# A router, eight experts and a gated layer on one core: the low parts of all expert weights move to VectorE, the conversion of the float64 weights gets a plan, and the last layer begins with two token groups in turn

## The chip, the cores and the metric

The kernel runs on one core of a Trainium2 chip. The metric is the device time of one launch in microseconds, the median of several runs. Lower is better.

## The reference

Three layers follow each other: attention in which keys far below the row's maximum are masked out, a mixture of eight experts that sends each token to one expert, and a gated feed-forward layer. All is fp32, but the three weights of the last layer arrive as float64, because their scaling makes numpy widen them.

```python
# attention: B=4, H=8, S=576, D=64        -> x [2304, 512]
scores = scale * q @ k.T ; keep scores >= max - tau ; attn = softmax ; attn @ v
# experts: N=2304 tokens, D=512, E=8, F=1024
expert_idx = argmax(normalized(x) @ normalized(emb).T / tau)
for e in range(E):                          # tokens of that expert only
    h = maximum(x[mask] @ w1[e], 0.0)       # w1 [8, 512, 1024]
    out[mask] = gate_w[mask, None] * (h @ w2[e])   # w2 [8, 1024, 512]
# last layer: d_ff = 1536, weights float64
g = x @ w_gate ; val = x @ w_val
return (g * sigmoid(g) * val) @ w_out
```

## The kernel before

TensorE multiplies in a rounded fp32 form (F32R). To keep fp32 accuracy each operand is split into a high part (the rounded value, a ScalarE cast) and a low part (operand minus high part, a subtraction on VectorE or GpSimd), and each product is three matmuls: high by high, high by low, low by high.

**Attention** takes the first third of the span; the change does not touch it. During it and behind it the router sorts the tokens by expert in DRAM (`xs`), and the first 256 tokens of one expert are already done (`Early`).

**Experts** (`moe`). The experts are taken by their number of remaining tokens, the fullest first: rank r = 0 to 7 has room for 448, 368, 336, 304, 288, 256, 256 and 256 tokens (`CW`). A rank has eight slots, k = 0 to 7, one for each 128 columns of the hidden layer. In slot k `l1(r, k)` makes one hidden tile (12 matmuls), ScalarE and VectorE cut it into `hh` and `hl`, and `l2(r, k - 2)` adds the tile of two slots earlier to the four outputs (12 matmuls). The weights come in pieces of two slots: `wload(1, q)` and `wload(2, q)` fetch 512 KB each into one of two buffers, and `wsplit` makes the parts. ScalarE casts the high part; the low part of every w1 piece and of the first w2 pieces is made by GpSimd, the low part of w2 from piece 12 on (and of piece 0) by VectorE. The next rank's tokens are transposed in slots 5 and 6 (`xT`), and results go out by `yout` and `stores`. The order here is that of the code (`manual_schedule`).

**Float64 weights** (`Weights2`). The last layer's weights are 36 blocks (gate, value, out for each of 12 columns of d_ff), fetched as pairs of 32-bit words, 512 KB each. `split` converts one to fp32: a ScalarE scale, then three VectorE operations that put the words together (tile `wb`). `join` makes its high part (ScalarE) and its low part (GpSimd). `turn(i)` does some of it in slot i of the experts: it starts a load in every second slot until 18 blocks are fetched. What is left is done by `step`, three times per step of the last layer.

**Last layer** (`moe2`). Six groups of 384 tokens. A step (g, k) is `l1(g, k)`, 24 matmuls of 384 columns into `pg` and `pv`, then Silu on ScalarE, the product on VectorE, its split into `uh` and `ul`; and `l2` of the step before, nine matmuls of 512 columns into three output tiles. The steps go group by group, k = 0 to 11 in each. Before the change no order is fixed here: the framework's scheduler chooses it on every engine. `pg` and `pv` share five PSUM banks, the outputs have three. All loads of the kernel go through one queue (SP), in order; a load that waits for its buffer holds up those behind it.

Of the kernel before, what the change touches and what calls it, by code (L numbers as in the profile page):

```python
# [15 lines left out]
def f(ap):  # L16
    return ap.bitcast(F32)
# [1140 lines left out]
def moe(ctx, tc, attn, hp, w1, w2, xs, ti, yd, idl, ident):  # L1158
# [24 lines left out]
    def gate(r, *ts):  # L1183
        for t in ts or range(0, CW[r], 128):
            gated((nc.scalar, nc.vector)[t // 128 % 2], st[r]["xw"][0:min(128, CW[r] - t), t // 128, :])

    def wload(nm, q):
        r, fp = divmod(q, 4)
        e, sl = bass.ds(st[r]["e"], 1), slice(256 * fp, 256 * fp + 256)
        if nm == 1:  # L1190
            t = pw.tile([128, 4, 256], F32, tag="w1", name="w1r")
            src = w1[e, :, sl].rearrange("e (c p) f -> p (e c) f", p=128)
        else:
            t = pw.tile([128, 2, DM], F32, tag="w2", name="w2r")
            src = w2[e, sl, :].rearrange("e (k p) d -> p (e k) d", p=128)
        nc.sync.dma_start(t[:], src)
        raw[nm, q] = t

    def wsplit(nm, q):
        t = raw.pop((nm, q))  # L1200
        hi = pwh.tile(list(t.shape), F32R, tag=f"{nm}h", name=f"w{nm}h")
        lo = pwh.tile(list(t.shape), F32R, tag=f"{nm}l", name=f"w{nm}l")
# [3 lines left out]
        W[nm, q] = (hi, lo)  # L1206

    def xT(r, c):

# [100 lines left out]
    wload(1, 0)  # L1310
    wload(2, 0)
    wload(1, 1)
    wsplit(1, 0)
    w2s, y0 = yield
    pxw, px, ph = p("m_xw", 1), p("m_x", 1), p("m_h", 3)
    pps, psy = p("m_ps", 4, space=PSUM), p("m_py", 4, space=PSUM)
    wload(2, 1)
    wsplit(2, 0)
    for i in range(8 * NE):
        r, k = divmod(i, 8)  # L1320
        q = 4 * r + k // 2
        if k == 0 and r + 1 < NE:
            regs(r + 1)
            xload(r + 1)
        if k == 4:
            ids(r)
            if r + 1 < NE:
                gate(r + 1)
# [33 lines left out]

class Weights2:

    EARLY = 6
    NF = DF2 // 128

    def __init__(self, ctx, tc, wg, wv, wo):
        self.tc, self.nc = tc, tc.nc
        p = lambda n, b: ctx.enter_context(tc.tile_pool(name=n, bufs=b, reuse_waits="tile", side="right"))  # L1370
        self.pw, self.pr = p("n_w", 1), p("n_r", 2)
        self.src = {"g": wg.bitcast(I32), "v": wv.bitcast(I32), "o": wo.bitcast(I32)}
        self.W = {}
        self.todo = [(k, nm) for k in range(self.NF) for nm in "gvo"]
        self.raw, self.half = [], []

    def turn(self, i):

        early = 3 * self.EARLY
        n = 3 * self.NF - len(self.todo)  # L1380
        if n < early and i % 2 == 0:
            self.load()
        if i % 2 == 1:
            self.join()
        elif len(self.raw) > 1 or n >= early:
            self.split()

    def step(self):
        if self.todo:
            self.load()  # L1390
        self.split()
        self.join()

    def load(self):
        k, nm = self.todo.pop(0)
        src = self.src[nm]
        if nm == "o":
            src = src[128 * k:128 * k + 128, :].rearrange("p (c f) -> p c f", c=4)
        else:
            src = src[:, 256 * k:256 * k + 256].rearrange("(c p) f -> p c f", p=128)  # L1400
        r = self.pr.tile([128, 4, 128, 2], I32, tag="r", name="r" + nm)
        self.nc.sync.dma_start(r[:].rearrange("p c f t -> p c (f t)"), src)
        self.raw.append((k, nm, r))

    def split(self):
        if not self.raw:
            return
# [3 lines left out]
        b = self.pr.tile([128, 512], I32, tag="wb", name="wb")  # L1411
        stt = nc.vector.scalar_tensor_tensor


        nc.scalar.activation(f(H), f(H), AF.Copy, scale=2.0 ** -112)
        nc.vector.tensor_scalar(b[:], L, 29, None, op0=ALU.logical_shift_right)  # L1416
        stt(out=b[:], in0=H, scalar=3, in1=b[:], op0=ALU.logical_shift_left, op1=ALU.bitwise_or)  # L1417
        stt(out=b[:], in0=H, scalar=-2 ** 31, in1=b[:], op0=ALU.bitwise_and, op1=ALU.bitwise_or)  # L1418
        self.half.append((k, nm, b))

    def join(self):
        if not self.half:
            return
# [13 lines left out]
def parts_y(pool):  # L1437
    return [pool.tile([128, 4, GT], F32R, tag="y" + x, name="y" + x) for x in "hl"]
# [7 lines left out]
def moe2(ctx, tc, w2s, yd, idl, out, y0, py0, pys):  # L1446
# [13 lines left out]

    H, Y = {}, {0: y0}

    def l1(g, k):
# [12 lines left out]
        s = pu.tile([128, GT], F32, tag="s", name="s")  # L1476
        nc.scalar.activation(s[:, 0:n], res[0][:, 0:n], AF.Silu)  # L1477
        nc.vector.tensor_tensor(s[:, 0:n], res[1][:, 0:n], s[:, 0:n], op=ALU.mult)  # L1478
        uh = pu.tile([128, GT], F32R, tag="uh", name="uh")
        ul = pu.tile([128, GT], F32R, tag="ul", name="ul")  # L1480
        nc.scalar.copy(uh[:, 0:n], s[:, 0:n])  # L1481
        nc.vector.tensor_tensor(ul[:, 0:n], s[:, 0:n], f(uh[:, 0:n]), op=ALU.subtract)
        H[g, k] = (uh, ul)

    O = {}

# [20 lines left out]
                in_=o[:], in_offset=None, bounds_check=NTOK - 1, oob_is_err=False)  # L1507
            apart(tc, "out", ins)

    seq = [(g, k) for g in range(len(groups)) for k in range(NF)]  # L1510
    for i, (g, k) in enumerate(seq):
        if w2s.todo:
            for _ in range(3):
                w2s.step()
        if g + 1 < len(groups):
            if k == 2:
                raw = pr.tile([128, 4, GT], F32, tag="yr", name="yr")
                nc.sync.dma_start(raw[:], yd[:, GT * (g + 1):GT * (g + 2)].rearrange("(c p) n -> p c n", p=128))
                Y[g + 1] = parts_y(py if g % 2 == 0 else py0)
            if k in (5, 6, 7, 8):  # L1520
                split_y(nc, Y[g + 1], k - 5, raw[:, k - 5, :])
        l1(g, k)
        if i:
            l2(*seq[i - 1])
            if seq[i - 1][1] == NF - 1:
                store(g - 1)
    l2(*seq[-1])
    store(len(groups) - 1)

# [35 lines left out]
def body(tc, q, k, v, tau, emb, mtau, w1, w2, wg, wv, wo, out):  # L1565
    nc = tc.nc
    with ExitStack() as top:
# [125 lines left out]
```

## Time and profile before

| | us |
|---|---|
| runs shown, median (lowest, highest) | 1085.92 (1081.8, 1086.0) |
| the profiled execution, its own time | 1089.41 |
| its span, first to last instruction | 1087.7 |
| granted TensorE clock over the span | 0.99 |
| TensorE busy | 1052.2 |
| VectorE, ScalarE, GpSimd busy | 583.1, 489.1, 375.0 |

Experts begin at 384.0 us of the span and the last layer at 625.3. Busy time of TensorE is modelled from pipelined matmuls, so a busy TensorE may still be slower than it could be; how far apart matmuls start tells more than how long one takes.

### The profile page before, as it was taken

To read this page: it belongs to the slowest core of one execution; us is meant where nothing else is said; L and a number is where in the kernel's file an instruction comes from. 1 tells how busy PE (TensorE), PEld (TensorE's weight loads), DVE (VectorE), ACT (ScalarE), POOL (GpSimd) and SP (SyncE) were. 2 spreads that over 40 slices of the span, in tenths; PEclk is the share of its full clock that TensorE was granted. 3 is DMA by queue.
4 is the path that set the end of the run, shared out by engine and by line. 5 is a ranking of instruction groups with operands and counts; after the bars stand their busy time and mean duration, and the time that the engine had idled before them with its cause. 6 is when DMAs were issued, how large, how long until landed. Compare 5 with 4: busy or idle time off the path is not lost.

```text
span 1087.7 us, 18328 instructions
## 1 busy us (share of the span) xinstructions
PE 1052.2 (97%) x6512; PEld 908.8 (84%) x6512; DVE 583.1 (54%) x1257; ACT 489.1 (45%) x1012; POOL 375.0 (34%) x414
## 2 busy tenths in 40 slices
PE   6999999999999689999999999999999999999997
PEld 5666676676668679999999998899999999999996
DVE  6877877888887335788964488421211211211211
ACT  5777777777773335565555454311211211211111
POOL 6444444455676355774643344110100100100101
PEclk9999999999999889999999999999999999999999
DMA  9678989755841477789897464100100100000000
GB/s 182 161 193 220 204 217 213 190 125 144 243 105 41 150 194 246 219 245 205 266 260 211 140 194 140 38 36 1 59 1 1 59 1 1 30 1 1 30 1 30
DMA packets 128574, 135.84 MB, mean 125 GB/s; under 512 B 52488, under 2 KB 94984, under 8 KB 128480
## 3 DMA queue, kind: packets, MB, share of 16 engines
q1 hardware_dynamic: 125600, 125.18, 43.4%
q0 software_dynamic: 2880, 9.46, 2.3%
q8 instruction: 53, 0.87, 0.3%
q14 instruction: 41, 0.34, 0.1%
HBM read 81.29 MB, written 27.77 MB: 100 GB/s over the span
## 4 chain that ended last, share of the span: by engine, by line
issue 39%; PE 11%; DMA 7%; POOL 3%; DVE 3%; ACT 1%; SPq 1%; POOLq 0%; ACTq 0%; DVEq 0%
PE ph L1248 5%; PE y L1266 5%; DMA w1r<-in_moe_w_dram 2%; DMA ro<-in_moe_w_out_dram 2%; DMA rg<-in_moe_w_gate_dram 2%; POOL w1l L1205 1%; POOL out_dram L1505 1%; DMA w2r<-in_moe_w_dram 1%; DVE wb L1417 1%; DMA rv<-in_moe_w_val_dram 1%; DVE wb L1418 1%; PE pxt L1217 1%; DVE wb L1416 0%; ACT w2h L1203 0%; POOL ol L1430 0%
## 5 line engine op out<-in xcount | busy, mean ns | idle before, releaser
L1478 DVE TENSOR_TENSOR s<-pv,s 128x384 f32<-128x384 f32 x72 | 40.1, 557 | 273.9 <-PE pv L1473 272.9
L1505 POOL DMA_INDIRECT out_dram<-os,idi x18 | 17.9, 994 | 378.2 <-DVE os L1503 374.5
L196 DVE TENSOR_REDUCE nmx<-PS 128x1 f32<-128x576 f32 x144 | 108.8, 756 | 58.1 <-PE PS L165 36.1
L1477 ACT ACTIVATE s<-pg 128x384 f32<-128x384 f32 x72 | 35.4, 491 | 181.4 <-PE pg L1473 181.4
L290 ACT COPY h<-PS 128x256 f32<-128x256 f32 (+2 forms) x176 | 67.2, 382 | 82.5 <-PE PS L247 81.1
L230 DVE SCALAR_TENSOR_TENSOR E<-PS,thr,E 128x576 f32<-128x576 f32 x128 | 103.5, 808 | 0.1
L1205 POOL TENSOR_TENSOR w1l<-w1r,w1h 128x1024 fp32r<-128x1024 f32 x32 | 80.8, 2525 | 52.1 <-ACT w1h L1203 52.1
L1481 ACT CAST uh<-s 128x384 fp32r<-128x384 f32 x72 | 37.0, 514 | 137.0 <-DVE s L1478 137.0
L220 ACT ACTIVATE E<-PS,nmx 128x576 f32<-128x576 f32 x128 | 96.4, 753 | 2.7 <-DVE nmx L196 0.8
L1473 PE MATMUL pg<-yh,gl 128*128 128x384 f32 x288 | 96.8, 336 | 0.0
L1473 PE MATMUL pg<-yh,gh 128*128 128x384 f32 x288 | 96.7, 336 | 0.0
L1473 PE MATMUL pg<-yl,gh 128*128 128x384 f32 x288 | 96.6, 336 | 0.0
L1473 PE MATMUL pv<-yh,vl 128*128 128x384 f32 x288 | 96.6, 335 | 0.0
L1473 PE MATMUL pv<-yh,vh 128*128 128x384 f32 x288 | 96.5, 335 | 0.0
L1473 PE MATMUL pv<-yl,vh 128*128 128x384 f32 x288 | 96.5, 335 | 0.0
L314 PE MATMUL y<-h,nv 128*64 128x320 f32 (+2 forms) x528 | 89.7, 422 | 0.0
L1496 PE MATMUL o<-oh,uh 128*128 128x512 f32 x216 | 85.0, 394 | 2.7 <-ACT uh L1481 2.7
L165 PE MATMUL PS<-KH,qs 128*128 128x288 f32 x256 | 86.1, 351 | 1.4 <-ACT h L290 1.2
L247 PE MATMUL PS<-ident,E 128*128 128x128 f32 x576 | 86.6, 277 | 0.6 <-DVE E L230 0.5
L1496 PE MATMUL o<-oh,ul 128*128 128x512 f32 x216 | 85.8, 397 | 0.0
L1496 PE MATMUL o<-ol,uh 128*128 128x512 f32 x216 | 85.3, 395 | 0.0
L247 PEld LDWEIGHTS PS<-ident,E 128*128 128x128 f32 x576 | 65.6, 140 | 22.3 <-issue 19.1
(328 smaller groups left out, 2577.2 us busy)
## 6 DMA issues: line engine op xcount, KB each, us to landing
w1r<-in_moe_w_dram SPq DMA_DIRECT2D x32, 512.0 KB, 6.5
w2r<-in_moe_w_dram SPq DMA_DIRECT2D x32, 512.0 KB, 5.1
xs<-zero SPq DMA_DIRECT2D x8, 1542.0 KB, 7.6
KH<-tkh SPq DMA_DIRECT2D x60, 144.0 KB, 2.6
KL<-tkl SPq DMA_DIRECT2D x60, 144.0 KB, 2.6
rg<-in_moe_w_gate_dram SPq DMA_DIRECT2D x12, 512.0 KB, 6.2
rv<-in_moe_w_val_dram SPq DMA_DIRECT2D x12, 512.0 KB, 8.3
ro<-in_moe_w_out_dram SPq DMA_DIRECT2D x12, 512.0 KB, 3.6
```

Source lines behind the costliest of these rows:

```text
L165: ins = nc.tensor.matmul(S[:, i, a:a + n], x, y, start=first, stop=last)
L196: nc.vector.tensor_reduce(nmx[:], S[:, :, 0:288], axis=AX.XY, op=ALU.max, negate=True)
L220: nc.scalar.activation(e, d["S", s][:, :, 0:288], AF.Exp, bias=d["nm", s][0][:], scale=1.0)
L230: nc.vector.scalar_tensor_tensor(out=e, in0=d.pop(("S", s))[:, :, 0:288], scalar=d.pop(("nm", s))[1][:], in1=e, op0=ALU.is_ge, op1=ALU.mul ...
L247: ins = nc.tensor.transpose(ps[:, o:o + 128], src, self.ident[:])
L290: self.tc.declare_no_dep(self.nc.scalar.copy(o, i).ins, group=f"new1_{g}", reason="the other bank")
L314: nc.tensor.matmul(ps[64 * b:64 * b + 64, p0:p1], v, self.H[i][:, k, o + p0:o + p1], start=c == 0, stop=c == 4 and (p1 == n or c0 == 0))
L1205: eng.tensor_tensor(lo[:], t[:], f(hi[:]), op=ALU.subtract)
L1248: nc.tensor.matmul(ps[:, 0:C], w[:, c, o:o + 128], x[:, c, 0:C], start=n == 0, stop=n == 11)
L1266: nc.tensor.matmul(d["y"][c][:, 0:C], w[:, k % 2, sl], h[:, 0:C], start=k == 0 and i == 0, stop=k == 7 and i == 2)
L1473: nc.tensor.matmul(ps[:, 0:n], w[:, c, :], y[:, c, 0:n], start=m == 0, stop=m == 11)
L1496: nc.tensor.matmul(O[g][t][:], u[:, sl], w[:].rearrange("p c f -> p (c f)"), start=k == 0 and i == 0, stop=k == NF - 1 and i == 2)
```

## The change

Three edits. (1) In `moe`, `wsplit` becomes `whigh` and `wlow`. The low parts are all VectorE's (but for the very first piece, which GpSimd still makes), and each is written a slot or a part of one behind its high part. The high part of the next w1 piece now stands behind `l1` of the slot, not ahead of it, and the next rank's gating stands behind both. (2) `Weights2` loads nothing in rank 0, keeps three blocks loaded ahead in a pool of their own with three buffers, and converts by plan: `begin` writes ScalarE's work on a block, `end` a slot later VectorE's. Two blocks in each of ranks 1 to 3 and one in each of ranks 4 to 7 are begun. In the last layer the same goes on, one block in even steps and two in odd ones, with the low parts on VectorE. (3) The last layer takes the first two groups in turn, two steps apart, so that each new block of weights serves two steps; its order on all engines is that of the code. `pg` and `pv` have two banks, the outputs six. A Silu of one column at the experts' end loads ScalarE's table ahead of time.

```diff
-    def wsplit(nm, q):
...
-        nc.scalar.copy(hi[:], t[:])
-        eng = nc.vector if (nm, q) == (2, 0) or nm == 2 and q >= 12 else nc.gpsimd
-        eng.tensor_tensor(lo[:], t[:], f(hi[:]), op=ALU.subtract)
+    def whigh(nm, q):
...
+            nc.scalar.copy(hi[:], t[:])
+    def wlow(nm, q, eng=nc.vector):
...
+            eng.tensor_tensor(lo[:], t[:], f(W[nm, q][0][:]), op=ALU.subtract)
...
+        if k % 2 == 0 and q + 2 < NQ:
+            wload(1, q + 2)
+        if k == 1:
+            wlow(1, q + 1)
+        l1(r, k)
         if k % 2 == 0:
-            if q + 2 < NQ:
-                wload(1, q + 2)
-            if q + 1 < NQ:
-                wsplit(1, q + 1)
-        l1(r, k)
+            whigh(1, q + 1)
+            wlow(2, q)
+        elif k > 1:
+            wlow(1, q + 1)
+        if k == 4 and r + 1 < NE:
+            gate(r + 1)
...
         if k % 2 == 1:
-            if q + 1 < NQ:
-                wsplit(2, q + 1)
+            whigh(2, q + 1)
...
+    nc.scalar.activation(one[:], ident[:, 0:1], AF.Silu)
     l2(NE - 1, 7)
...
     def turn(self, i):
+        r, k = divmod(i, 8)
+        if r and k % 4 == 0:
+            self.fill()
+        if r and k % 4 > 1 and (k < 4 or r < 4):
+            if k % 2 == 0:
+                self.begin(1)
+            else:
+                self.end()
...
+    def begin(self, n):
+        for _ in range(n):
+            if self.half:
+                self.high()
+            if self.raw:
+                self.scale()
...
-        nc.gpsimd.tensor_tensor(flat(lo), f(b[:]), f(flat(hi)), op=ALU.subtract)
+        self.lows.append(lambda: nc.vector.tensor_tensor(flat(lo), f(b[:]), f(flat(hi)), op=ALU.subtract))
...
-    pps, pso = p("n_ps", 5, space=PSUM), p("n_po", 3, space=PSUM)
+    pps, pso = p("n_ps", 2, space=PSUM), p("n_po", 6, space=PSUM)
...
         nc.scalar.activation(s[:, 0:n], res[0][:, 0:n], AF.Silu)
+        w2s.begin(1 + i % 2)
         nc.vector.tensor_tensor(s[:, 0:n], res[1][:, 0:n], s[:, 0:n], op=ALU.mult)
...
+        w2s.end()
+        w2s.fill()
...
-    seq = [(g, k) for g in range(len(groups)) for k in range(NF)]
+    LAG = 2
+    seq = [(0, k) for k in range(LAG)]
+    for k in range(NF):
+        seq += [(g, k + LAG - LAG * g) for g in range(2) if k + LAG - LAG * g < NF]
+    yload(1)
+    for c in range(4):
+        do[seq.index((1, 0)) - 2 + c // 2].append((ysplit, 1, c))
...
+            ctx.enter_context(tc.manual_schedule())
             moe2(ctx, tc, w2s, yd, idl, out, y0, py0, c)
```

VectorE in rank 7, the last expert, before the change (`hl` is the low part of a hidden tile, `w2l` that of a w2 piece; L1205 is `wsplit`):

```order
L1253 SCALAR_TENSOR_TENSOR hl<-ph,hh 128x256
L1205 TENSOR_TENSOR w2l<-w2r,w2h 128x1024
L1253 SCALAR_TENSOR_TENSOR hl<-ph,hh 128x256 x2
L1205 TENSOR_TENSOR w2l<-w2r,w2h 128x1024
L1253 SCALAR_TENSOR_TENSOR hl<-ph,hh 128x256 x2
```

And after it, from slot 1 to slot 4 of that rank (`w1l` is the low part of a w1 piece, `ol` that of a converted block, `wb` the three operations that put a block's words together; L1210 is `wlow`):

```order
L1210 TENSOR_TENSOR w1l<-w1r,w1h 128x1024
L1258 SCALAR_TENSOR_TENSOR hl<-ph,hh 128x256 x2
L1210 TENSOR_TENSOR w2l<-w2r,w2h 128x1024
L1258 SCALAR_TENSOR_TENSOR hl<-ph,hh 128x256
L1210 TENSOR_TENSOR w1l<-w1r,w1h 128x1024
L1459 TENSOR_TENSOR ol_8229<-wb,oh_8228 128x512
L1446 TENSOR_SCALAR wb<-rg 128x512
L1447 SCALAR_TENSOR_TENSOR wb<-rg,wb 128x512
L1448 SCALAR_TENSOR_TENSOR wb<-rg,wb 128x512
L1258 SCALAR_TENSOR_TENSOR hl<-ph,hh 128x256
```

The low part of w1 has come to VectorE; in slot 3 it stands right behind `hl` of that slot, ahead of a block's conversion, and the hidden tile of slot 4 comes behind the conversion.

ScalarE at the seam between experts and last layer before the change (`hh` and `ysb` are the experts' last hidden tiles and outputs, `s<-pg` the Silu, `yh<-yr` the high part of the next group's tokens):

```order
L1252 ACTIVATE hh<-ph 128x256 x2
L1273 COPY ysb<-y 128x256 x2
L1429 CAST gh_8556<-wb 128x512
L1429 CAST vh_8567<-wb 128x512
L1477 ACT_TABLE_LOAD
L1477 ACTIVATE s<-pg 128x384
L1429 CAST oh_8578<-wb 128x512
L1429 CAST gh_8622<-wb 128x512
L1481 CAST uh<-s 128x384
L1477 ACTIVATE s<-pg 128x384
L1442 CAST yh<-yr 128x384 x4
```

And after it:

```order
L1257 ACTIVATE hh<-ph 128x256 x2
L1370 ACT_TABLE_LOAD
L1370 ACTIVATE one<-ident 128x1
L1278 COPY ysb<-y 128x256 x2
L1506 ACTIVATE s<-pg 128x384
L1458 CAST gh_8504<-wb 128x512
L1441 ACTIVATE rv<-rv 128x512
L1511 CAST uh<-s 128x384
L1471 CAST yh<-yr 128x384 x2
L1506 ACTIVATE s<-pg 128x384
L1458 CAST vh_8554<-wb 128x512
```

The table load has moved ahead of the experts' last copies, and two casts of group 1's tokens (`yh`), which wait for a load of `yd`, now stand ahead of the second Silu.

## Rows read from the trace of the kernel before

**Rows 1.** The page: busy us (share of the span) x instructions of each engine.

```profile
PE 1052.2 (97%) x6512; PEld 908.8 (84%) x6512; DVE 583.1 (54%) x1257; ACT 489.1 (45%) x1012; POOL 375.0 (34%) x414
```

**Rows 2.** Who TensorE waited for, 384 to 690 us: total, times, longest.

```profile
PE o L1496 <- ACT uh L1481: 2.7, 4, 0.7
PE ph L1248 <- POOL w1l L1205: 1.7, 3, 1.2
PE y L1266 <- DVE hl L1253: 1.1, 1, 1.1
PE pxt L1217 <- DVE hl L1253: 0.7, 1, 0.7
PE y L1266 <- ACT hh L1252: 0.5, 1, 0.5
```

**Rows 3.** Last layer by stretches: PE busy (matmuls), granted clock, DMA share, GB/s.

```profile
625.30:702.60 77.30, 74.62 (x389) 1.00 0.39 123
702.60:777.70 75.10, 75.10 (x397) 1.00 0.06 22
```

**Rows 4.** Timeline, rank 3: start, duration, what; in brackets the idle before it.

```profile
501.75 2.56 POOL L1205 TENSOR_TENSOR w1l<-w1r,w1h 128x1024 fp32r<-128x1024 f32 x1
502.18 2.68 DVE L1417 SCALAR_TENSOR_TENSOR wb<-rg,wb 128x512 int32<-128x512 int32 x1
504.36 0.82 PE L1248 MATMUL ph<-xh,w1l 128*128 128x304 f32 x4 [1.20 <-POOL w1l L1205]
```

**Rows 5.** Timeline, end of rank 4.

```profile
545.41 0.68 ACT L1415 ACTIVATE rg<-rg 128x512 f32<-128x512 f32 x1 [5.96 <-DMA rg<-in_moe_w_gate_dram]
548.20 1.77 DVE L1418 SCALAR_TENSOR_TENSOR wb<-rg,wb 128x512 int32<-128x512 int32 x1
550.38 0.40 PE L1266 MATMUL y<-hl,w2h 128*128 128x288 f32 x1 [1.13 <-DVE hl L1253]
```

**Rows 6.** Stretches around it: busy of PE, PEld, DVE, ACT, POOL, then clock.

```profile
546.60:552.30 5.70, 4.12 (x26) 3.67 (x25) 5.35 (x7) 3.94 (x9) 4.59 (x2) 0.92 0.79 231
552.30:554.90 2.60, 2.60 (x15) 2.60 (x14) 2.46 (x5) 1.65 (x2) 0.88 (x1) 0.52 0.85 278
```

**Rows 7.** Lines L1205 and L1417: duration ns min/median/max, first and last start.

```profile
L1205 POOL TENSOR_TENSOR w1l<-w1r,w1h x32: 2352/2488/2854, 378.7 to 613.3; 128x1024 fp32r<-128x1024 f32 x32
L1205 DVE TENSOR_TENSOR w2l<-w2r,w2h x21: 1214/1226/3430, 381.6 to 618.0; 128x1024 fp32r<-128x1024 f32 x21
L1417 DVE SCALAR_TENSOR_TENSOR wb<-rg,wb x12: 673/693/2699, 399.6 to 675.7; 128x512 int32<-128x512 int32 x12
```

**Rows 8.** Stretches of ranks 4 and 7, columns as in rows 6.

```profile
521.00:553.00 32.00, 29.07 (x205) 27.54 (x204) 27.98 (x35) 18.43 (x34) 17.81 (x8) 0.98 0.83 256
601.00:625.00 24.00, 24.00 (x206) 24.00 (x205) 9.62 (x16) 9.95 (x18) 8.31 (x4) 1.00 0.44 116
```

**Rows 9.** Timeline, rank 7, from the end of a hidden tile to the next one's w1l.

```profile
615.43 0.28 PE L1266 MATMUL y<-hh,w2h 128*128 128x256 f32 x1
616.04 0.42 DVE L1253 SCALAR_TENSOR_TENSOR hl<-ph,hh 128x256 fp32r<-128x256 f32 x1 [2.05 <-ACT hh L1252]
617.77 0.64 PE L1248 MATMUL ph<-xh,w1l 128*128 128x256 f32 x4
```

**Rows 10.** Tile w1r, the loads of w1 pieces: issue to landing.

```profile
DMA to landing us min/median/max: 4.5/6.5/9.9
```

**Rows 11.** Timeline at the start of the last layer.

```profile
628.51 0.40 SPq L1518 DMA_DIRECT2D yr<-yd  x1
628.52 1.28 ACT L1477 ACT_TABLE_LOAD   x1 [1.97 <-DMA yd<-ysb]
633.32 1.74 ACT L1442 CAST yh<-yr 128x384 fp32r<-128x384 f32 x4
```

**Rows 12.** Last layer, 625 to 710 us, by line: count, busy us, mean ns.

```profile
L1429 ACT CAST gh<-wb 128x512 fp32r<-128x512 f32 x6 | 3.7, 620 | 5.4 <-DVE wb L1418 5.4
L1482 DVE TENSOR_TENSOR ul<-s,uh 128x384 fp32r<-128x384 f32 x13 | 7.2, 557 | 2.4 <-ACT uh L1481 2.4
```

More of the change, by code (lines that the diff above doesn't have):

```diff
@@ L1197, in wload @@
         raw[nm, q] = t
-    def wsplit(nm, q):
-        t = raw.pop((nm, q))
-        hi = pwh.tile(list(t.shape), F32R, tag=f"{nm}h", name=f"w{nm}h")
-        lo = pwh.tile(list(t.shape), F32R, tag=f"{nm}l", name=f"w{nm}l")
-        nc.scalar.copy(hi[:], t[:])
-        eng = nc.vector if (nm, q) == (2, 0) or nm == 2 and q >= 12 else nc.gpsimd
-        eng.tensor_tensor(lo[:], t[:], f(hi[:]), op=ALU.subtract)
-        W[nm, q] = (hi, lo)
+    def whigh(nm, q):
+        if q < NQ:
+            t = raw[nm, q]
+            hi = pwh.tile(list(t.shape), F32R, tag=f"{nm}h", name=f"w{nm}h")
+            nc.scalar.copy(hi[:], t[:])
+            W[nm, q] = [hi]
+    def wlow(nm, q, eng=nc.vector):
+        if q < NQ:
+            t = raw.pop((nm, q))
+            lo = pwh.tile(list(t.shape), F32R, tag=f"{nm}l", name=f"w{nm}l")
+            eng.tensor_tensor(lo[:], t[:], f(W[nm, q][0][:]), op=ALU.subtract)
+            W[nm, q].append(lo)
     def xT(r, c):
@@ L1312, in moe @@
     wload(1, 1)
-    wsplit(1, 0)
+    whigh(1, 0)
+    wlow(1, 0, nc.gpsimd)
     w2s, y0 = yield
+    one = p("m_1", 1).tile([128, 1], F32, name="one")
     pxw, px, ph = p("m_xw", 1), p("m_x", 1), p("m_h", 3)
@@ L1317, in moe @@
     wload(2, 1)
-    wsplit(2, 0)
+    whigh(2, 0)
     for i in range(8 * NE):
@@ L1363 @@
 class Weights2:
-    EARLY = 6
+    EARLY = 3
     NF = DF2 // 128
@@ L1374, in __init__, with fill, end @@
         self.todo = [(k, nm) for k in range(self.NF) for nm in "gvo"]
-        self.raw, self.half = [], []
+        self.raw, self.half, self.lows, self.words = [], [], [], []
+    LOADED = 3
     def turn(self, i):
-        early = 3 * self.EARLY
-        n = 3 * self.NF - len(self.todo)
-        if n < early and i % 2 == 0:
-            self.load()
[L1383 to L1392, printed above, removed]
+        r, k = divmod(i, 8)
[6 more added lines that the diff above has]
+                self.end()
+    def fill(self):
+        while self.todo and len(self.raw) < self.LOADED:
+            self.load()
+    def begin(self, n):
[4 more added lines that the diff above has]
+                self.scale()
+    def end(self):
+        for todo in (self.lows, self.words):
+            while todo:
+                todo.pop(0)()
     def load(self):
@@ L1400, in load, with scale @@
             src = src[:, 256 * k:256 * k + 256].rearrange("(c p) f -> p c f", p=128)
-        r = self.pr.tile([128, 4, 128, 2], I32, tag="r", name="r" + nm)
+        r = self.p3.tile([128, 4, 128, 2], I32, tag="r", name="r" + nm)
         self.nc.sync.dma_start(r[:].rearrange("p c f t -> p c (f t)"), src)
         self.raw.append((k, nm, r))
-    def split(self):
-        if not self.raw:
-            return
+    def scale(self):
         nc = self.nc
@@ L1410, in split, with words, high @@
         L, H = (r[:].rearrange("p c f t -> p (c f) t")[:, :, x] for x in range(2))
-        b = self.pr.tile([128, 512], I32, tag="wb", name="wb")
-        stt = nc.vector.scalar_tensor_tensor
         nc.scalar.activation(f(H), f(H), AF.Copy, scale=2.0 ** -112)
[L1416 to L1423, printed above, removed]
+        def words():
+            b = self.pr.tile([128, 512], I32, tag="wb", name="wb", bufs=3)
+            stt = nc.vector.scalar_tensor_tensor
+            nc.vector.tensor_scalar(b[:], L, 29, None, op0=ALU.logical_shift_right)
+            stt(out=b[:], in0=H, scalar=3, in1=b[:], op0=ALU.logical_shift_left, op1=ALU.bitwise_or)
+            stt(out=b[:], in0=H, scalar=-2 ** 31, in1=b[:], op0=ALU.bitwise_and, op1=ALU.bitwise_or)
+            self.half.append((k, nm, b))
+        self.words.append(words)
+    def high(self):
         nc = self.nc
@@ L1461, in moe2, with l1 @@
     H, Y = {}, {0: y0}
-    def l1(g, k):
+    def l1(g, k, i):
         n = groups[g][1]
@@ L1475, in l1 @@
             res.append(ps)
-        s = pu.tile([128, GT], F32, tag="s", name="s")
+        s = pu.tile([128, GT], F32, tag="s", name="s", bufs=1)
         nc.scalar.activation(s[:, 0:n], res[0][:, 0:n], AF.Silu)
+        w2s.begin(1 + i % 2)
         nc.vector.tensor_tensor(s[:, 0:n], res[1][:, 0:n], s[:, 0:n], op=ALU.mult)
@@ L1508, in store, with yload, ysplit @@
             apart(tc, "out", ins)
-    seq = [(g, k) for g in range(len(groups)) for k in range(NF)]
-    for i, (g, k) in enumerate(seq):
[L1512 to L1522, printed above, removed]
+    raw = {}
+    def yload(g):
+        raw[g] = pr.tile([128, 4, GT], F32, tag="yr", name="yr")
+        nc.sync.dma_start(raw[g][:], yd[:, GT * g:GT * (g + 1)].rearrange("(c p) n -> p c n", p=128))
+    def ysplit(g, c):
+        if c == 0:
+            Y[g] = parts_y(py if g % 2 else py0)
+        split_y(nc, Y[g], c, raw[g][:, c, :])
+    LAG = 2
+    seq = [(0, k) for k in range(LAG)]
+    for k in range(NF):
+        seq += [(g, k + LAG - LAG * g) for g in range(2) if k + LAG - LAG * g < NF]
+    do = defaultdict(list)
+    yload(1)
+    for c in range(4):
+        do[seq.index((1, 0)) - 2 + c // 2].append((ysplit, 1, c))
+    n = seq.index((0, NF - 1))
+    do[n - 3].append((yload, 2))
+    for c in range(4):
+        do[n + 1 + c // 2].append((ysplit, 2, c))
+    for g in range(2, len(groups)):
+        n = len(seq)
+        seq += [(g, k) for k in range(NF)]
+        if g + 1 < len(groups):
+            do[n + 2].append((yload, g + 1))
+            for c in range(4):
+                do[n + 5 + c].append((ysplit, g + 1, c))
+    for i, (g, k) in enumerate(seq):
+        for what, *x in do[i]:
+            what(*x)
+        l1(g, k, i)
         if i:
```

5 lines of the change are left out of this document (2 added, 3 removed).

## The prediction

> **What bounds the kernel now.** The page's shares come first [rows 1]: TensorE is busy for 97% of the span and the other engines for about half of it or less. So what the others spend costs nothing by itself; only the places count where TensorE waits for them. The change leaves the number and sizes of matmuls alone, so I read the waits of TensorE from the start of the experts to the end of the conversion [rows 2], then stretches for what these waits cost, then the timeline at two of them for their cause.
>
> The last layer gives the price of a wait [rows 3]. A full group of twelve steps takes 75.10 us, 6.26 a step. Its `l1` has 24 x 384 columns and its `l2` 9 x 512, so `l2` is a third, 2.09 us, and `l1` 4.17. The first group lacks one `l2`, so it should take 73.0 us; it takes 77.3. That is 4.3 us for four waits for `uh` whose idle time is 2.7 us [rows 2]: a wait costs its idle time and 0.4 us more for the emptied pipeline.
>
> The experts have six waits with 1.7 + 1.1 + 0.7 + 0.5 = 4.0 us of idle time [rows 2]; with 0.4 each that is 6.4 us. After the longest, TensorE runs 2.6 us at a granted clock of 0.52 and has 0.92 over the 5.7 us before it [rows 6]; the first is near its lower level (1.2 of 2.4 GHz) after TensorE had stood idle, and costs about 1.2 + 0.5 us. Sum 8.1 us. The cause stands in the timeline. In rank 3 [rows 4] TensorE waits for `w1l`, which GpSimd needs 2.56 us for, and beside it a VectorE operation takes 2.68 us that takes 0.69 in the median [rows 7]. At the end of rank 4 [rows 5] ScalarE stands 5.96 us before the scale of a float64 block whose load is late, the casts of the experts' weights stand behind it in its queue, then VectorE's `wb` takes 1.77 us, and `hl` comes 1.13 us too late. Rank 7, which loads no more blocks, has no wait at all [rows 8].
>
> So **12.4 us** (8.1 + 4.3) is what the change can take away. Nothing else on TensorE's path moves: attention and the start of the experts keep their order.
>
> **Low parts on VectorE.** 31 w1 pieces and 11 w2 pieces (32 less VectorE's 21) leave GpSimd [rows 7]. The trace has no w1 low part on VectorE; the nearest row is w2's, of the same shape [rows 7]: 1.21 us at least, 1.23 in the median, 3.43 at most. I take 1.23, as even with GpSimd at work half of them took that; 3.43 is the upper bound. The difference, 2.2 us, is near one GpSimd subtraction (2.49), so VectorE's long operations are those that stood against GpSimd, and GpSimd will do no more low parts beside them.
>
> Is VectorE then in time? The tightest place is a rank of 256 tokens. There `hl` ends 1.03 us after the hidden tile's last matmul gives way to `l2` (615.43, 616.04 + 0.42) [rows 9], and TensorE asks for the next w1 piece's low part 2.34 us after it (617.77). In slots 3 and 5 the low part now stands right behind `hl`: 1.03 + 1.23 = 2.26 us, 0.08 us to spare, which a hand-over of semaphores uses up. With more tokens the 20 matmuls between take longer (448 tokens: 4.1 us by columns), so ranks 0 to 3 have 0.5 us or more. In slot 3 a conversion stands behind the low part, its words three operations of up to 0.69 us and its low part about 0.6 (half of 1.23); it pushes `hl` of slot 4 back by about 1.6 us and what follows in slot 5 by some tenths. I count 0.3 us a rank for ranks 5 to 7: **0.9 us lost**. Without the free GpSimd, so with operations of up to 3.43 us, this cover is gone (the third rival).
>
> One piece of advice speaks against this edit. In the stretch of rank 4 VectorE is busy for 27.98 of 32 us [rows 8], and four more low parts of 1.23 us make 32.9. The Trainium skill (Perfetto Trace Analysis, Optimizing Scalar/DVE Operations) says that a saturated DVE is a reason to hand work to ScalarE or even GPSIMD, and adds that this might not help as DVE and GPSIMD share a read port. By the rows the engine is not full: the 27.98 us contain the time in which operations stood against GpSimd, and rank 7, with as many low parts on VectorE but no blocks, needs 9.62 of 24 us. It stands as a rival below.
>
> **Planned conversion.** Before, 18 of 36 blocks are done in the experts, as six of each kind come later [rows 12]; now nine are, so nine times a scale, a cast, three word operations leave this stage, and their nine GpSimd low parts. The loads stand ready three ahead, one to five slots before their scale, so the 5.96 us of [rows 5] have no successor. The cover is that lead; a load of a block that lands later than 10 us would put it back. For w1 pieces the lead is shorter: a piece's buffer is free when its low part is done, its cast is due some 5.8 us later at 256 tokens (two slots of 2.83 us and the tile, less 1.3 for `hl`, low part and issue) and may slip by 1.8 before `hh` stands behind it. Landing takes 6.5 us in the median and 9.9 at most [rows 10]: normally free, at worst 2.3 us for one piece. I take **1 us** for a few such pieces, between nothing and the 4.0 us of today's idle time.
>
> **Last layer.** 27 blocks are left instead of 18. Three blocks per two steps need on VectorE 4 x 0.56 for product and `ul` [rows 12] and 3 x (up to 3 x 0.69 + 0.6) for blocks, 10 us of 12.5; on ScalarE under 7 us. Before it was three blocks per step, 6 us and more of VectorE's 6.26, and `uh` came late. In an odd step `uh` stands behind two scales and two casts of 0.62 us [rows 12], about 1.1 us after `pv`; TensorE wants it 6.26 us after. A block is needed two steps after its conversion. So the four waits go, **4.3 us**.
>
> Two banks for `pg` and `pv` are free of charge while Silu ends within the 4.17 us in which TensorE does `pv` and the `l2` before. At the seam this is close. The first Silu waited for the last stores of `yd` to be read, until 628.52, behind the table load [rows 11]; the next `pg` is due at 625.3 + 4.17 = 629.5, and Silu takes half a us: 0.5 us to spare, as the table load no longer stands between. The second Silu now stands behind two casts of group 1's tokens. Their load was issued at 628.51 and the casts ran from 633.32 [rows 11]; two casts and Silu end at 634.7, and the third step's `pg` wants its bank at 625.3 + 2 x 4.17 + 2.09 = 635.7. One us to spare, so nothing is charged; the cover gone costs each us of lateness in full.
>
> **Sum.** 12.4 - 0.9 - 1.0 = 10.5 us off 1089.4, the profiled execution's own time: 1078.9. That execution is 3.5 us above the median of the runs shown. If the 3.5 us lie in things that the change does not touch, the median becomes 1075.4; if they were longer waits than usual, the gain at the median is 7 us and it becomes 1079. I say **1076.5**.
>
> **Rivals.**
> *The experts' waits are the loads'.* For it: DMA share 0.83 in rank 4, the 5.96 us wait, landings up to 9.9 us. Against it: rank 7 runs without waits on loads of the same size, and fewer blocks are fetched. Then 4.3 us and about a third of 8.1 are gained, 7 in all at most, 5 at the median: 1081.
> *Group 1's tokens come late.* The casts hold Silu up. With a landing 5 us later (9.9 instead of 4.8, as the slowest w1 piece [rows 10]) TensorE waits 4 us once, and Silu's lateness passes on to no other step: 10.5 less 4, so the median comes 4 us above the forecast: 1080.5.
> *The low parts on VectorE come late (slower).* If w1's low part takes L, TensorE waits 1.03 + L - 2.34 x tokens / 256 at slots 4 and 6 (0.3 less there, for the transposes). With L = 3.43 that is 2.1 and 1.8 us in each rank of 256 and 23 us over all eight, 10.6 more than is gained: 1096. With L = 2.49 it is 9.6 us, and nothing changes. It decides for slower from L = 3.0 us on. Only contention that GpSimd did not cause could do this.
> *VectorE is full.* The advice weighed above, with its price from [rows 8]: four more low parts make 32.9 us of work in rank 4's 32, so the experts keep their 8.1 us and ranks 3 and 4 grow by 0.9 each; 4.3 - 1.8 leaves 2.5 us: 1083.5. Against it is rank 7's 9.62.
> *No change.* The waits had another cause than conversion and low parts, and come back elsewhere: 1086. The stalls sit where those operations are, which speaks against it.
>
> **How the numbers follow.** Forecast 0.65 (1073 to 1080), loads 0.14, group 1 late 0.06, VectorE full 0.04, late low parts 0.07, no change 0.04. From about 1070.5 (all 12.4 us and 3 us of scatter, as the lowest run lies 4 below the median) to 1083 holds eight in ten: above it lie the late low parts, no change, VectorE full, and little else. Half a per cent, 5.4 us, is about what a measurement of this kernel tells from no change, as the runs shown differ by 4.2. Faster than 1080.5: the forecast, and half of the loads' and of group 1's case, less the forecast's edge, 0.73. Within: 0.19. Slower: 0.08.
>
> **What would show it.** Right: waits of `ph`, `y`, `pxt` and `o` in the experts and the last layer below 1.5 us together, no stretch at a low clock behind rank 1, VectorE's low parts at 1.2 to 1.3 us throughout, GpSimd idle from 385 us on but for the output, the first 24 steps of the last layer in 24 x 6.26 - 2.1 = 148 us. Wrong: `ph` waiting for VectorE's `w1l` at slots 4 and 6, ScalarE waiting for w1 loads, a gap before the third `pg` of the last layer.

## The result, and the profile after

The changed kernel takes 1074.49 us in the median of six runs (1073.59 to 1076.55), the kernel before 1083.32 beside it: ratio 0.9918, 95% interval 0.9898 to 0.9939, 8.8 us less. On a later occasion it took 1079.18 us beside 1085.59, 6.4 us less by the medians, ratio 0.9934 (0.9920 to 0.9949). Forecast were 1076.5 us and 9.4 us less.

The page after, answering to [rows 1], then who TensorE waited for from 384 to 690 us, answering to [rows 2]:

```profile
PE 1046.3 (98%) x6512; PEld 905.9 (84%) x6512; DVE 592.0 (55%) x1335; ACT 489.0 (46%) x1013; POOL 214.6 (20%) x336
```

```profile
PE pxt L1222 <- DVE xw L1072: 1.0, 2, 0.5
```

Five lines of waits with 6.7 us have become one with 1.0, and it is a new one: a matmul of TensorE is about to transpose the next rank's tokens and waits until VectorE has gated them. VectorE's low parts after, to be held against [rows 7] (duration in ns min/median/max, first and last start):

```profile
L1210 DVE TENSOR_TENSOR w2l<-w2r,w2h x32: 1211/1215/1224, 384.7 to 607.8; 128x1024 fp32r<-128x1024 f32 x32
L1210 DVE TENSOR_TENSOR w1l<-w1r,w1h x31: 1208/1215/1220, 385.8 to 605.0; 128x1024 fp32r<-128x1024 f32 x31
```

The maximum fell from 3.43 to 1.22 us. Three stretches after: rank 4, which lies earlier here than in [rows 8], and the last layer's first twelve and first 24 steps (columns as there):

```profile
513.53:540.08 26.55, 26.55 (x202) 26.26 (x201) 18.76 (x29) 14.65 (x25) 0.00 (x0) 1.00 0.74 217
```

```profile
613.93:687.20 73.27, 73.27 (x389) 68.63 (x388) 51.95 (x93) 33.24 (x64) 0.00 (x0) 1.00 0.44 133
613.93:762.32 148.39, 148.39 (x785) 138.88 (x784) 92.45 (x164) 57.67 (x111) 2.94 (x3) 1.00 0.35 107
```

In all three TensorE is busy without a gap at a clock of 1.00. Rank 4 took 31.4 us before and takes 26.6; VectorE, which makes more low parts in it and converts fewer blocks, is busy for 18.76 us of it, where it had 27.98 of the 32 us in [rows 8]. The first twelve steps of the last layer took 77.30 us [rows 3] and take 73.27.

To compare kernels I cut each profiled execution at three matmuls: the first of the experts, the first of the last layer, the first of its last 18 (behind that every kernel has 11.6 us). Microseconds:

| kernel | experts begin at | experts | last layer |
|---|---|---|---|
| before, first profile | 384.0 | 241.3 | 450.8 |
| before, again | 384.3 | 238.7 | 450.3 |
| after, first profile | 379.0 | 235.0 | 446.7 |
| after, again | 383.4 | 235.3 | 446.5 |
| low parts on VectorE alone | 383.8 | 239.7 | 450.5 |
| two groups alone | 382.4 | 241.2 | 452.3 |
| these two together | 383.0 | 239.7 | 451.7 |
| after, low parts of w1, w2 on GpSimd | 382.9 | 245.1 | 446.4 |
| after, scheduler's order in the last layer | 377.8 | 241.9 | 450.3 |
| after, one group | 380.3 | 235.8 | 504.5 |
| after, w1's low part twice | 382.6 | 252.7 | 446.4 |
| after, low parts earlier | 384.5 | 233.3 | 446.4 |
| after, conversion's low parts on GpSimd | 379.1 | 233.2 | 446.4 |

First profile against first: experts 6.3 us shorter, last layer 4.1. Another 5.0 us lie ahead of the experts, where no line was changed. Their start goes with the occasion and not with the edits: 382.4 to 384.5 us in the eight executions of two occasions, where the kernel before took 1086.41 and 1085.59 us, and 377.8 to 380.3 in the three of another (scheduler's order, one group, conversion's low parts on GpSimd), where it took 1082.55.

### The profile page after: what moved, and what is told of

It is laid out like the page before. It is cut to its first block, busy times and chain, and to the rows that moved or that the text cites. A ratio compares the mean times of both kernels' runs of the same rounds, so it can differ in the third digit from the quotient of the medians.

```text
span 1072.2 us, 18202 instructions
## 1 busy us (share of the span) xinstructions
PE 1046.3 (98%) x6512; PEld 905.9 (84%) x6512; DVE 592.0 (55%) x1335; ACT 489.0 (46%) x1013; POOL 214.6 (20%) x336
## 4 chain that ended last, share of the span: by engine, by line
issue 63%; POOL 1%; POOLq 0%
POOL out_dram L1537 1%; POOLq L1745 0%; POOLq L1083 0%; POOLq L1537 0%
## 5 line engine op out<-in xcount | busy, mean ns | idle before, releaser
L1508 DVE TENSOR_TENSOR s<-pv,s 128x384 f32<-128x384 f32 x72 | 40.1, 556 | 247.2 <-PE pv L1502 233.3
L1271 PE MATMUL y<-hh,w2h 128*128 128x256 f32 (+5 forms) x256 | 79.5, 310 | 0.0
```

Source lines behind the costliest of these rows:

```text
L1271: nc.tensor.matmul(d["y"][c][:, 0:C], w[:, k % 2, sl], h[:, 0:C], start=k == 0 and i == 0, stop=k == 7 and i == 2)
```

## The experiments

The theory: the experts had two causes of stalls, (A) GpSimd's low parts, which are late and hold VectorE, and (B) blocks whose late load holds ScalarE; the last layer had (C) three blocks to a step. Rivals: one cause does it all; VectorE is now nearly full.

**Before, unchanged, once more.**

> The kernel before, unchanged, profiled a second time. In the two profiles at hand the experts begin at 384.0 us before the change and at 379.0 after it, though no instruction ahead of them has changed. If that is scatter between executions, this profile begins the experts anywhere from 379 to 384 us and may differ from the first by some us; if the change causes it, this one begins at 383 to 385 us. Both expect 240 to 243 us for the experts (first matmul of rank 0 to first matmul of the last layer; 241.3 in the first profile) and 450 to 452 us from there to the last 18 matmuls (450.8).

1086.61 us beside a median of 1086.41. The experts take 238.7 us, less than the 240 to 243 expected. The long waits of the experts differ from one execution to the next: rank 4 took 31.4 us in the first profile and 28.3 here, while the last layer differs by 0.5. The stages thus promise 3.4 + 3.8 = 7.2 us against this profile of before and 10.2 against the first, both from the repeated profile of after.

**Low parts on VectorE alone** (kernel before).

```diff
-        eng = nc.vector if (nm, q) == (2, 0) or nm == 2 and q >= 12 else nc.gpsimd
+        eng = nc.gpsimd if (nm, q) == (1, 0) else nc.vector
```

> The kernel before with one edit: VectorE makes every low part of the expert weights but the very first, at the place in the code where GpSimd made them. Theory A (the experts' waits come from VectorE and GpSimd standing against each other): the experts take 236 to 238 us instead of 241.3, most of what the full change gains there (235.0), and the ratio to before is about 0.996. Theory B (they come from block loads and weight loads that hold ScalarE's queue up, so the plan and the later place are what counts): the low parts now hold VectorE up behind casts that wait for their loads, the experts take 241 to 246 us and nothing is gained. Conversion low parts stay on GpSimd here, so some contention is left under A: up to 1 us.

1086.1 us, ratio 1.000 (0.9987 to 1.0014). The experts' 239.7 us lie between the ranges of the two theories. GpSimd's waits are gone, and one wait of 4.2 us stands in rank 4. Its timeline (start, duration, what; in brackets the idle before):

```profile
541.38 0.70 ACT L1415 ACTIVATE rg<-rg 128x512 f32<-128x512 f32 x1 [5.31 <-DMA rg<-in_moe_w_gate_dram]
541.39 0.43 DVE L1416 TENSOR_SCALAR wb<-rg 128x512 int32<-128x512 int32 x1 [4.75 <-DMA rg<-in_moe_w_gate_dram]
542.34 0.45 DVE L1253 SCALAR_TENSOR_TENSOR hl<-ph,hh 128x288 fp32r<-128x288 f32 x1
542.84 1.11 PE L1217 MATMUL pxt<-ident,xw 128*128 128x128 f32 x4 [4.20 <-DVE hl L1253]
```

ScalarE and VectorE both stand for the load of one block, and `hl` and the transposes behind them. That is (B) as in [rows 5], with (A) taken away: taking (A) away alone gains nothing.

**The changed kernel with the low parts back on GpSimd** (all of w1, and w2's that were there; planned conversion and two groups stay).

```diff
     def wlow(nm, q, eng=nc.vector):
+            eng = nc.vector if (nm, q) == (2, 0) or nm == 2 and q >= 12 else nc.gpsimd
```

> The changed kernel with one part undone: the low parts go back to the engine that had them before (GpSimd for w1 and for w2 pieces 1 to 11), at their new place. Theory A: the waits come back, the experts take 239 to 243 us instead of 235.0, with w1l waits of TensorE at slots 4 and 6, since the late place leaves 2.3 us and the subtraction takes 2.5. Theory B: the experts take 235 to 236.5 us. The last layer stays at 446.7 us under both.

1088.54 us, ratio to before 1.0023 (1.0008 to 1.0038). The last layer keeps its gain (446.4), the experts are 10 us longer than after's. Who TensorE waited for, and one of the places:

```profile
PE pxt L1223 <- DVE xw L1072: 6.6, 4, 2.0
PE ph L1254 <- POOL w1l L1211: 1.4, 3, 0.5
```

```profile
562.11 3.19 POOL L1211 TENSOR_TENSOR w1l<-w1r,w1h 128x1024 fp32r<-128x1024 f32 x1 [2.83 <-ACT w1h L1203]
563.01 2.58 DVE L1072 TENSOR_SCALAR xw<-xw 128x512 f32<-128x512 f32 x1
565.64 0.55 PE L1223 MATMUL pxt<-ident,xw 128*128 128x128 f32 x3 [2.02 <-DVE xw L1072]
```

The gating takes 0.48 us in the changed kernel and 2.58 here, beginning while GpSimd subtracts and ending just after it; the other three that TensorE waits for take 2.58 to 2.60. So in this kernel (A) acts less by GpSimd's own lateness (1.4 us) than by what it holds on VectorE (6.6). The theory expected 239 to 243 us and waits for `w1l` at slots 4 and 6; it was 245.1 us, and the three waits for `w1l` came at slot 2.

**Two groups alone** (kernel before, with two of eight banks for `pg` and `pv`, one or two blocks a step).

```diff
-        if w2s.todo:
-            for _ in range(3):
+        if w2s.todo or w2s.raw or w2s.half:
+            for _ in range(1 + i % 2):
...
```

> The kernel before with one edit in the last layer: the first two groups in turn, with two and six PSUM banks, and one block converted in even steps and two in odd ones; everything else, the scheduler and the low parts on GpSimd too, as before. If the halved need for blocks is what takes the four waits away, the last layer takes 446.5 to 447.5 us instead of 450.8 and the ratio is about 0.996. If it is the order written by hand or the low parts on VectorE, it stays at 449 to 451. The experts stay at 240 to 243 us.

1088.13 us, ratio 1.002 (1.0005 to 1.0034). The last layer takes 452.3 us, above both ranges of the expectation: the waits for `uh` are gone, and three for the Silu with 2.9 us of idle time have come.

**The two together**, the diffs of the last two runs.

> The kernel before with two of the three edits: all low parts but the first on VectorE (at their old place, not a step later), and the last layer begun with two token groups by turns; the conversion of the float64 weights stays as it was, and the scheduler orders the last layer. Alone the first gave experts 239.7 and last layer 450.5 us, the second 241.2 and 452.3. Theory 'in the last layer the two groups need only a VectorE that nobody holds': the 2.9 us of pg on the first Silu go, last layer 446.7 to 448 us; experts 239.7 us, since ScalarE is still held by the late load of a block; ratio to the kernel before 0.995 to 0.997. Rival 'the last layer needs the planned conversion or the order by hand': last layer 450 to 452 us, ratio 0.999 to 1.001.

1088.88 us, ratio 1.0027 (1.0014 to 1.0040): the experts as with the first edit alone, the last layer 451.7, so the rival holds. Its timeline:

```profile
665.12 1.67 DVE L1418 SCALAR_TENSOR_TENSOR wb<-rv,wb 128x512 int32<-128x512 int32 x1
666.83 0.62 ACT L1429 CAST vh<-wb 128x512 fp32r<-128x512 f32 x1 [1.97 <-DVE wb L1418]
667.35 0.48 ACT L1477 ACTIVATE s<-pg 128x384 f32<-128x384 f32 x1
667.89 0.44 PE L1473 MATMUL pg<-yh,gh 128*128 128x384 f32 x1 [1.85 <-ACT s L1477]
```

The Silu, for whose bank TensorE waits, stands in ScalarE's queue behind the cast of a block whose words VectorE has not finished. With five banks for `pg` and `pv`, in the kernel before, no matmul waits for the Silu. The planned conversion makes the words a step ahead of their cast. Behind this wait TensorE runs for a while at the lower of its two clocks, so the last layer loses more than the 2.6 us of idle time (2 us of it, columns as above):

```profile
670.00:672.00 2.00, 2.00 (x7) 2.00 (x7) 1.90 (x5) 1.46 (x3) 0.00 (x0) 0.50 0.01 3
```

**The changed kernel, last layer in the scheduler's order.**

```diff
-            ctx.enter_context(tc.manual_schedule())
             moe2(ctx, tc, w2s, yd, idl, out, y0, py0, c)
```

> The changed kernel, but the scheduler and not the code's order puts the last layer's instructions in their queues. Theory 'with two PSUM banks the Silu must stand at its place in ScalarE's queue': the scheduler puts casts that wait for VectorE ahead of it, TensorE waits 2 to 4 us in the first steps, last layer 448.5 to 451 us as in the two kernels with two groups and the old conversion (452.3, 451.7); ratio to the changed kernel 1.002 to 1.004. Rival 'it is the conversion a step apart that does it, in whichever order': last layer 446.4 to 447 us, ratio 1.000.

1084.86 us, ratio to before 1.0028 (1.0008 to 1.0049). The last layer behaves as the first theory says (450.3, three waits for the Silu, 2.9 us). Unforeseen, the experts take 241.9. ScalarE's waits from 384 to 620 us, and the first of these places:

```profile
ACT rv L1441 <- DMA rv<-in_moe_w_val_dram: 6.0, 1, 6.0
ACT ro L1441 <- DMA ro<-in_moe_w_out_dram: 5.3, 1, 5.3
ACT rg L1441 <- DMA rg<-in_moe_w_gate_dram: 3.7, 1, 3.7
```

```profile
554.20 0.65 ACT L1223 CAST xs<-pxt 128x256 fp32r<-128x256 f32 x2 [0.60 <-PE pxt L1222]
560.80 0.67 ACT L1441 ACTIVATE rv<-rv 128x512 f32<-128x512 f32 x1 [5.96 <-DMA rv<-in_moe_w_val_dram]
561.37 1.03 ACT L1203 CAST w2h<-w2r 128x1024 fp32r<-128x1024 f32 x1
```

Before the last layer begins, 14 blocks have been scaled where the changed kernel has 10: the scheduler pulls scales of the last layer into the experts' ScalarE queue, where each waits for a load that has only just been issued, with the experts' casts behind it. All else is as in the changed kernel, so this is (B) by itself: 6.6 us (241.9 for 235.3).

The kernel before has the same cause. There `turn` fetches 18 blocks, the last of them issued at 529.04 us, but 22 have been scaled when the last layer begins. The block that held ScalarE for 5.96 us in [rows 5] is the 19th, a block of the last layer that the scheduler pulled forward; its load:

```profile
535.51 0.38 SPq L1402 DMA_DIRECT2D rg<-in_moe_w_gate_dram  x1
```

In the five profiles with the old conversion ScalarE waits 4.6 to 6.0 us for the 19th block and at most 0.7 us for any of the 18 before it. In the seven profiles with the last layer in the code's order no scale in the experts waits for its load. So the plan does not end (B) without the order by hand. Whether the order would do it without the plan was not run.

**One group.**

```diff
-        w2s.begin(1 + i % 2)
+        w2s.begin(3)
...
-    seq = [(0, k) for k in range(LAG)]
-    for k in range(NF):
-        seq += [(g, k + LAG - LAG * g) for g in range(2) if k + LAG - LAG * g < NF]
+    seq = [(g, k) for g in range(2) for k in range(NF)]
...
```

> The changed kernel with the last layer begun with one token group, as before: three blocks of the float64 weights have to be converted in each of the first group's steps, 27 in nine steps, where the changed kernel spreads them over 18. Theory 'the two groups carry the conversion': VectorE needs 3 x (1.77 + 1.2) for the blocks and 1.1 for the step's own work, 10 us, or 8.3 us where the parts run at their shortest, against a step of 6.25 us: 18 to 34 us more in the last layer, all in the first group, with TensorE waiting for gl, vl and ol; ratio to the changed kernel 1.017 to 1.033. Rival 'the conversion runs ahead far enough in any order, and the two groups only cost or save a wait': last layer 447 to 451 us, ratio 1.000 to 1.004.

1134.7 us, ratio to before 1.0486 (1.0463 to 1.0509): the direction of the theory, but 58 us more in the last layer for its 18 to 34. Eight steps take 11.9 to 14.4 us. The stretch of most of them, and ScalarE's waits in 630 to 740 us:

```profile
640.00:700.00 60.00, 40.76 (x148) 34.18 (x146) 35.50 (x62) 19.39 (x35) 0.00 (x0) 0.74 0.41 123
```

```profile
ACT vh L1458 <- DVE wb L1448: 24.4, 8, 3.0
ACT rv L1441 <- DMA rv<-in_moe_w_val_dram: 23.7, 8, 3.1
ACT ro L1441 <- DMA ro<-in_moe_w_out_dram: 11.9, 8, 1.7
ACT rg L1441 <- DMA rg<-in_moe_w_gate_dram: 7.6, 7, 1.4
```

VectorE, which I had made the bound, is busy for 35.5 of 60 us. Three raw buffers hold one step's blocks, so each step waits for its own loads, then for its words, and TensorE, idle in between, runs at a clock of 0.74. So two groups let the plan's three buffers suffice; one group with more buffers was not run. The experts keep their gain (235.8).

**w1's low part twice.** The subtraction is done twice into the same tile.

```diff
-            eng.tensor_tensor(lo[:], t[:], f(W[nm, q][0][:]), op=ALU.subtract)
+            for _ in range(2 if nm == 1 and q else 1):
+                eng.tensor_tensor(lo[:], t[:], f(W[nm, q][0][:]), op=ALU.subtract)
```

> The changed kernel with the low part of each w1 piece but the first made twice, one instruction of 1.22 us behind the other on VectorE, into the same tile: nothing is computed otherwise, the price L of a low part becomes 2.43 us. Theory 'the chain of slots 3 and 5 decides' (hl at +1.03 us, low part done at 1.03 + L, TensorE asks at 2.34 us x tokens/256): each of ranks 5 to 7 loses 2 x 1.1 us, rank 4 2 x 0.8, rank 3 2 x 0.7, together 9.7 us, in waits of ph on w1l at slots 4 and 6 and nowhere else; ratio to the changed kernel 1.009. Rival 'VectorE is full': at 256 tokens a rank it would be busy 17.2 of 25 us plus 6 or 7 times 1.22, some 25 of 25, and the loss grows by what follows late (hl, the gate of the next rank, the conversion), 12 to 18 us, with waits on xw and y too. Rival 'there is slack that I did not count': 0 to 3 us.

1095.66 us where the changed kernel had 1079.18 in the same session: 16.5 us more, 17.4 in the experts. Waits, and two places in rank 7:

```profile
PE ph L1254 <- DVE w1l L1211: 13.7, 15, 1.5
PE pxt L1223 <- DVE xw L1072: 1.4, 3, 0.6
```

```profile
610.68 0.75 DVE L1279 COPY ysb<-y 128x256 f32<-128x256 f32 x2
611.34 2.48 DVE L1211 TENSOR_TENSOR w1l<-w1r,w1h 128x1024 fp32r<-128x1024 f32 x2
613.87 0.74 PE L1254 MATMUL ph<-xh,w1l 128*128 128x256 f32 x4 [1.34 <-DVE w1l L1211]
617.90 0.43 DVE L1259 SCALAR_TENSOR_TENSOR hl<-ph,hh 128x256 fp32r<-128x256 f32 x1 [1.28 <-ACT hh L1258]
618.24 2.47 DVE L1211 TENSOR_TENSOR w1l<-w1r,w1h 128x1024 fp32r<-128x1024 f32 x2
620.77 0.50 PE L1254 MATMUL ph<-xh,w1l 128*128 128x256 f32 x2 [0.96 <-DVE w1l L1211]
```

The lower place, slot 4, is the one I had priced at 1.1 us: 0.96. At slot 6 it appears in rank 7 alone; in the other ranks the transposes stand between. The upper one, slot 2, I had missed: in slot 1 the low part stands behind the copies of the last rank's `y`, and it is the tighter place (1.34). Over all ranks seven waits there make 7.8 of the 13.7 us. The waits on `xw` grew by 0.4 us only, so the rival 'VectorE is full' is not what cost the time, although 17 us lies in its range. In the changed kernel itself, with L = 1.22, the low part of slot 1 is already a little late: in ranks 5 to 7 TensorE's weight loads wait 0.2 to 0.3 us for it.

**Low parts earlier.** In slots 3 and 5 the low part ahead of `hl`, the gating one step earlier.

```diff
+            if r + 1 < NE:
+                gate(r + 1)
...
-        if k == 1:
+        if k % 2:
             wlow(1, q + 1)
...
-        elif k > 1:
-            wlow(1, q + 1)
-        if k == 4 and r + 1 < NE:
-            gate(r + 1)
```

> The changed kernel with the low part of the next w1 piece put ahead of the first matmuls' evacuation (hl) in slots 3 and 5 as it already is in slot 1, and with the gating of the next rank's tokens put one step earlier in slot 4. Theory 'what is left of the waits hangs on the order in VectorE's queue': the waits pxt on xw (1.0 us in 2) and of ph on w1l (0.7 us in 3) go, experts 233.3 to 234.0 instead of 235.0 us, ratio to the changed kernel 0.9985 to 0.999. Rival 'VectorE is then held at the low part until ScalarE's high part is there, and hl comes late': the wait goes over to y on hl, experts 235 to 238 us, ratio 1.000 to 1.003.

1076.49 us, ratio to before 0.9907 (0.9892 to 0.9922), the changed kernel beside it 1079.18. From 386 to 690 us no matmul waits; the weight loads' 0.7 us for `w1l`, which the theory wanted gone, stay. Ranks 4 to 6 are 0.3, 0.8 and 0.7 us shorter, the experts 2.1. Both edits went in together, so their shares stay open. The intervals of the two kernels touch; the stage shows the difference better than the total.

**Conversion's low parts on GpSimd.**

```diff
-        self.lows.append(lambda: nc.vector.tensor_tensor(flat(lo), f(b[:]), f(flat(hi)), op=ALU.subtract))
+        self.lows.append(lambda: nc.gpsimd.tensor_tensor(flat(lo), f(b[:]), f(flat(hi)), op=ALU.subtract))
```

> The changed kernel with the low parts of the converted float64 blocks, all 36, on GpSimd at their new place; the low parts of w1 and w2 stay on VectorE. Theory 'GpSimd hurts only where its low part is on the path or holds VectorE at a tight place': in the last layer VectorE has 2.5 us to spare in two steps and gives 3 x 1.2 us away, so its words may be stretched (0.69 to 1.5 us) without harm, last layer 446.4 to 447.5 us; in the experts the nine early ones (1.3 us each) may hold hl or the gate, 235 to 237 us; ratio to the changed kernel 1.000 to 1.003. Rival 'any work on GpSimd is dear': waits of TensorE for the Silu in the first 24 steps as in the kernels with two groups alone, last layer 449 us or more, ratio 1.003 to 1.006.

1073.02 us, ratio to before 0.9916 (0.9899 to 0.9933). The last layer is unmoved (446.4), and the experts are *shorter* than the changed kernel's, 233.2: no matmul waits in them either. Less stands ahead of the gating in VectorE's queue; w1's low parts stand where they did, so this speaks for the gating as the place of the 2 us and not for slots 3 and 5. So GpSimd is not dear in itself; it depends on what VectorE does beside it.

## Why the prediction was right

- **Experts, 8.1 us to be had.** Right: 6.3 us came (first profiles), and about 2 us were still left; with the low parts earlier the experts are 8.0 us shorter than in the execution I summed. The 8.1 belong to that one execution; between the two repeated ones the gain is 3.4.
- **The late block load.** That it would have no successor came true, but not by the lead of three blocks that I gave as the reason. The block was one of the last layer's that the scheduler pulled into the experts, and with the lead but without the order by hand such waits are there again (6.0, 5.3 and 3.7 us).
- **Low parts at 1.23 us.** 1.215, none above 1.224. The 3.43 us of [rows 7] were GpSimd's doing: they went with it, and 2.58 us came back for the gating when it returned.
- **0.9 us for slots 3 and 5, 1 us for late loads.** The sum, 1.9, is near the 2.1 that was left, and that is luck: the places were not these. The only idle waits of TensorE's matmuls were for the gating (two, 1.0 us), which the change moves behind a conversion and a low part in slot 4, and which I left out of the parts. The longest wait of ScalarE for a w1 load was 2.3 us (four waits, 5.0 us): one of my signs of being wrong, but no matmul waited for them.
- **The price of a late low part.** I had 9.6 us for a low part of 2.49 us, at slots 4 and 6. Made twice, at 2.48 us, it costs the experts 17.4 us: slot 2, which I put at nothing, has more than half of the idle time.
- **VectorE full.** This rival did not come: VectorE is busy for 18.76 of rank 4's 26.55 us, a smaller share than before [rows 8]. The Trainium skill (Perfetto Trace Analysis, Optimizing Scalar/DVE Operations) says that handing work of a saturated DVE to ScalarE or even GPSIMD may make sense, but that between DVE and GPSIMD it might not help. The trace agrees with the second half: handing the low parts back costs 10 us of the experts.
- **Last layer 4.3 us.** 4.1, and its first 24 steps take 148.4 us against 148. The seam was tighter than said: the first Silu ends at 618.18, 0.1 us after the next `pg` was due, not 0.5 before, and the first two steps take 4.31 and 6.37 us instead of 4.17 and 6.26.
- **The offset.** 1075.4 if the 3.5 us lay elsewhere, 1079 if they were longer waits. Both play a part, as the start differs by up to 6.7 us and rank 4 by 3 between executions. That 1076.5 came within 2.0 us of the result is in part luck: the kernel before was at 1083.32 beside it and not at 1085.92. The gain, which does not hang on that, was 8.8 and 6.4 us for 9.4.
- **The parts added up.** The sum treats low parts, plan and groups as if each brought its share. It held for all three together, but no experiment with only one or two of them beat the kernel before: 1.000 (low parts), 1.002 (groups), 1.0027 (these two), 1.0023 (plan and groups), 1.0486 (low parts and plan, three blocks to a step). With one cause of a stall gone, another one ended last. The plan alone and the order by hand alone were not run.

## What to carry to other kernels

When engines take turns at a stage, list every cause that ends a wait within a step's length: removing one of two can give nothing at all. Put an operation that waits for a transfer or another engine's chain into an in-order queue only when that is due to have ended, and check what stands behind it, since that is what the wait holds up. Where a scheduler orders a stage, look in the trace for work of that stage among the instructions of the one before. Busy time of an engine that another can hold up is no measure of its room: look at minimum and maximum of one operation first.

## What the runs showed of the hardware

- VectorE operations that ran beside a GpSimd subtraction were stretched or not by where their operands lie. With the conversion's low parts on GpSimd, the product `s`, which reads PSUM and SBUF, kept its time over the last layer, though 17 of these 25 ran beside a subtraction for 0.1 to 0.6 us; `ul`, which reads two tiles of SBUF, doubled at its longest, and all nine that ran beside one were stretched:

```profile
L1508 DVE TENSOR_TENSOR s<-pv,s x25: 545/557/558, 616.7 to 764.9; 128x384 f32<-128x384 f32 x25
```

```profile
L1512 DVE TENSOR_TENSOR ul<-s,uh x24: 557/559/1178, 617.8 to 759.7; 128x384 fp32r<-128x384 f32 x24
```

The Trainium skill (SBUF — State Buffer, Who interferes with whom) says that a DVE instruction with two SBUF inputs contends with a GpSimd instruction that reads SBUF, and one with at most one does not unless it runs in a mode with two ports. The trace agrees for both; that the gating (one tile, 0.48 to 2.58 us) belongs to such a mode would fit, and no run here tests it.

- Which of the two began first counts too. The `w2l` of 3.43 us in [rows 7] began at 492.61, 0.4 us behind a GpSimd subtraction. With the low parts back on GpSimd, 20 of VectorE's 21 `w2l` ran beside a subtraction, each of them began ahead of it, and none was stretched:

```profile
L1211 DVE TENSOR_TENSOR w2l<-w2r,w2h x21: 1215/1215/1217, 388.9 to 621.9; 128x1024 fp32r<-128x1024 f32 x21
```

- A wait costs more than its idle time, but not a fixed amount. With w1's low part twice, 16 waits more cost 17.4 us for 14.1 of idle time, 0.2 each where I had taken 0.4, and the granted clock stays at 1.00 behind them. With low parts and groups together, two waits of 0.7 and 1.85 us cost the last layer 5.2 us (451.7 for 446.5): behind the second one TensorE runs at 0.50 from 668.9 to 672.4 us, which is 1.7 us of it.
